# Integer addition in the conversion of 64-bit weights: DeltaNet and SwiGLU on one NeuronCore

## The chip, the cores and the metric

The kernel runs on one core of one Trainium2 chip. The metric is the device time of one launch in microseconds. A core has five engines with queues of their own: TensorE (PE in the profile; its weight loads are PEld), VectorE (DVE), ScalarE (ACT), GpSimd (POOL) and SyncE (SP), which only issues DMAs here.

## The reference

```python
def _attn_ref(q, k, v, beta):                  # q, k, v: (4, 8, 768, 48), beta: (4, 8, 768)
    k_n = k / (np.linalg.norm(k, axis=-1, keepdims=True) + 1e-06)
    state = np.zeros((B, H, D, D))
    for t in range(S):
        y[:, :, t] = np.einsum('bhd,bhde->bhe', q[:, :, t], state)
        v_old = np.einsum('bhde,bhd->bhe', state, kt)
        state = state + bt * np.einsum('bhd,bhe->bhde', kt, vt - v_old)

def _moe_ref(x, w_gate, w_val, w_out, rms_g):  # x: (3072, 384), d_ff = 1536
    rms = np.sqrt(np.mean(x * x, axis=-1, keepdims=True) + 1e-06)
    xn = x / rms * rms_g
    g = xn @ w_gate
    return (g / (1 + np.exp(-g)) * (xn @ w_val)) @ w_out
```

The output of the attention, with the heads of a token put side by side, is `x`. The three weight matrices arrive as 64-bit floats and are used as 32-bit ones, so the kernel has to convert 18 tiles of 768 numbers in each of 128 partitions. q, k, v and beta are 32-bit.

## The kernel before

**Chunks.** The sequence is cut into 12 chunks of 64 steps (`C = 64`), with all 32 heads and both halves of the batch in one chunk. The recurrence within a chunk becomes the inverse of a triangular matrix, built from products of keys. Per chunk, `norms`, `prep`, `qpart` and `recur` do this:

- `norms`: squares (ScalarE), sums (L557, VectorE), a root by power on POOL (L560), the reciprocal (VectorE). L629 scales the keys, on VectorE in chunk 0 and on POOL behind it.
- `prep`: transposes of the keys, their products (L538), a copy to DRAM (`dkk`) and a reload as `at`, in which each partition holds one block of a triangle. `scale` (L654) multiplies it by beta; 15 steps of a product and a sum (L701, L707) invert it. The result goes to DRAM (`dx`, from the buffer `wsum` in the first two chunks) and returns as `mt` and `x2bd`. Matmuls at L759, L783 and L807 merge the halves of the inverse, with copies such as L772 to `m1bd` between them.
- `recur`: products with the state (L849), the new values (L895), the output (L909), the state's update (L946), the root mean square of the output (L977, L983, and on POOL L995 and L996), its scaling (L1011), the transposes to `xf` or `xp1` (L1017) and their copies (L1021).

The first ffn matmul of chunk 0 is at L1084. For chunks 0 and 1 `ffn_plain` multiplies by the weights (L1084 up, L1066 down). For the other ten chunks the up product goes through fewer products of combined factors (L1177, with the combinations in `extra` and `w_in`), and L1234 does the down product. L1334 issues fillers: matmuls without a result, which the planner puts into TensorE's idle time before the time `until`.

**The weights.** `weights` puts 18 tiles into the plan, in order n = 0 to 17: gate and val tiles of `w_in` and tiles of `wo_sb`. A DMA on SP loads tile n into one of three buffers (`raw[n % 3]`), which lie in the large tile `more`. Even n are converted through parts of `xf` and `tmp`, odd n through parts of `more`. With `low` and `high` the two 32-bit halves of a 64-bit float:

- L465, ScalarE: `high` is read as a 32-bit float, scaled and put through Prelu into `top`.
- L453, VectorE: the bits of `top` are shifted left by three.
- L456, VectorE: sign and exponent of that are cut out into `cc`.
- L461, VectorE: `low` (an integer) times 2^-52 times `cc`, which is what the lower half adds.
- the sum of `top` and `cc`. For n below `NPE = 3` TensorE adds the two by matmuls with the identity (L478, L479) and ScalarE copies the result out of PSUM (L483). For the others VectorE adds them (L486).

**The order of the work.** Nothing above is issued in the order of the code. `Plan.add` notes each step with its engine, an assumed duration, a priority, and the keys that it reads and writes. `Plan.run` then simulates all queues 60 times (`forward`), takes new priorities from a pass from the end (`backward`) plus a little noise, keeps the best order, and issues the steps in it. Banks of PSUM and the fillers are assigned in that order too. The weight DMAs have due times of their own (`after`, in L444). DMAs of chunk 0's `prep` are spread over ScalarE's and SP's queues (L645, L649, and `turns` at L730); those of chunk 1 go to SP alone. An engine's queue runs in the planned order and waits at every step for what it needs. So whatever changes a step's engine or assumed duration can move any other step.

## Time and profile before

| what | value |
|---|---|
| timed runs | 711.06, 712.31, 715.30 us (median 712.31) |
| profiled execution, span from first to last instruction | 711.6 us |
| mean granted TensorE clock of the profiled execution | 0.995 |
| busy: TensorE, VectorE, ScalarE, POOL | 98%, 77%, 45%, 19% |
| first ffn matmul, L1084 | 74.01 us |
| conversion of weights, first Prelu to last sum | 13.0 to about 143.9 us |
| L453, L456, L461, L486 on VectorE, each of 128x768 | 0.55, 0.56, 0.96, 0.955 us |
| L465 on ScalarE | 0.93 us |

The page lists no time of the profiled execution other than its span; the shortest timed run is 0.5 us shorter than it and the median 0.7 us longer. Busy shares are of the whole span. The stages differ: up to 74 us only the inversions, the first products and the fillers run, and from there to the end matmuls of the ffn and of later chunks follow one another. Times are from the start of the span.

### The profile page before, as it was taken

Reading aid. Unit: us, or ns where it says so; the run is one execution under the profiler, and the core shown is the slowest. Engines: PE = TensorE matmul, PEld = TensorE weight load, DVE = VectorE, ACT = ScalarE, POOL = GpSimd, SP = SyncE. Lnnn points to the kernel's source line nnn. Section 1 sums busy time; section 2 is a strip of 40 time slices with the busy share of each in tenths; the row PEclk is TensorE's granted clock in tenths of the full one; section 3 lists DMA queues with packets and bytes.
Section 4 is the critical chain, followed back from the end, with each engine's and each line's share of the span. In section 5 each row is a group of like instructions: output and inputs, shape, how many; then the busy total and the mean of one; then the engine's idle time right before and its main releaser. Section 6 shows DMA issues by size and latency. Waiting matters only on the chain.

```text
span 711.6 us, 23292 instructions
## 1 busy us (share of the span) xinstructions
PE 698.8 (98%) x10036; PEld 634.8 (89%) x10036; DVE 545.9 (77%) x1139; ACT 317.7 (45%) x755; POOL 135.4 (19%) x140
## 2 busy tenths in 40 slices
PE   8998998999999999999999999999999999999997
PEld 5656777777799999999999999999999998999997
DVE  4899998999648959938959948946969847976473
ACT  5435553334244445546435355345355355234441
POOL 4201203102021232223130405005040304000000
PEclk9999998999999999999999999999999999999999
DMA  7777895431351261271161262154161161040000
GB/s 138 214 156 179 221 247 137 59 62 35 51 103 25 47 111 34 55 125 34 30 114 25 46 120 51 26 99 85 17 113 17 37 99 33 13 65 2 23 1 23
DMA packets 210071, 54.67 MB, mean 77 GB/s; under 512 B 199216, under 2 KB 202288, under 8 KB 209968
## 3 DMA queue, kind: packets, MB, share of 16 engines
q1 hardware_dynamic: 205120, 52.26, 36.8%
q10 hardware_dynamic: 4848, 0.92, 0.8%
q8 instruction: 79, 1.29, 0.7%
q14 instruction: 24, 0.20, 0.1%
HBM read 40.83 MB, written 12.32 MB: 75 GB/s over the span
## 4 chain that ended last, share of the span: by engine, by line
PE 89%; DVE 6%; DMA 2%; POOL 1%; ACT 1%; issue 1%; POOLq 0%; ACTq 0%; DVEq 0%
PE bank L1177 38%; PE bank L1234 20%; PE bank L1084 9%; PE bank L1066 4%; PE bank L849 3%; PE bank L538 3%; PE bank L515 3%; PE bank L909 2%; DVE acc L707 2%; PE bank L895 2%; PE bank L1334 1%; PE bank L1017 1%; DVE acc L701 1%; PE bank L946 1%; PE bank L783 1%; PE bank L807 1%
## 5 line engine op out<-in xcount | busy, mean ns | idle before, releaser
L1187 DVE TENSOR_TENSOR tmp<-tmp,bank 128x512 f32<-128x512 f32 x180 | 122.2, 685 | 88.6 <-PE bank L1177 63.0
L1177 PE MATMUL bank<-xf,w_in 128*128 128x128 f32 x1440 | 182.0, 277 | 0.0
L1177 PEld LDWEIGHTS bank<-xf,w_in 128*128 128x128 f32 x1440 | 170.1, 192 | 2.6 <-issue 1.2
L1177 PE MATMUL bank<-xf,more 128*128 128x128 f32 x960 | 123.9, 277 | 0.0
L1177 PEld LDWEIGHTS bank<-xf,more 128*128 128x128 f32 x960 | 115.1, 192 | 1.5 <-issue 0.4
L1189 ACT COPY tmp<-bank 128x512 f32<-128x512 f32 x120 | 68.7, 584 | 65.4 <-PE bank L1177 57.2
L707 DVE TENSOR_REDUCE acc<-acc 128x30 f32<-128x90 f32 (+4 forms) x180 | 85.0, 472 | 6.2
L1193 ACT ACTIVATE tmp<-tmp 128x256 f32<-128x256 f32 x120 | 49.5, 417 | 74.5 <-DVE tmp L1187 74.0
L701 DVE TENSOR_TENSOR acc<-acc,at 128x60 f32<-128x60 f32 (+4 forms) x180 | 63.1, 351 | 2.6
L1234 PE MATMUL bank<-wo_sb,hf 128*128 128x192 f32 x360 | 63.9, 328 | 0.0
L1194 DVE TENSOR_TENSOR hf<-tmp 128x256 f32<-128x256 f32 x120 | 53.9, 463 | 12.6 <-ACT tmp L1193 11.4
L560 POOL TENSOR_TENSOR knrm<-ksum,half 128x16 f32<-128x16 f32 x12 | 36.5, 3043 | 121.3 <-DVE ksum L559 121.3
L1234 PEld LDWEIGHTS bank<-wo_sb,hf 128*128 128x128 f32 x360 | 58.1, 190 | 0.5 <-DVE hf L1194 0.2
L1334 PE MATMUL bank<-ident 128*128 128x128 f32 (+2 forms) x156 | 45.2, 437 | 1.4 <-POOL ident masks.py:199 1.4
L1334 PEld LDWEIGHTS bank<-ident 128*128 128x128 f32 x156 | 26.3, 197 | 18.9 <-issue 16.4
L654 POOL TENSOR_TENSOR at<-at,beta_b 128x1024 f32<-128x1024 f32 x8 | 18.9, 2364 | 117.0 <-DMA at<-dkk 94.7
L728 POOL COPY acc<-acc 128x128 f32<-128x128 f32 x40 | 16.5, 445 | 129.2 <-DVE acc L707 128.5
L1084 PE MATMUL bank<-xf,w_in 128*128 128x256 f32 x144 | 33.6, 384 | 0.5 <-ACT xf L1021 0.5
L1084 PE MATMUL bank<-xp,w_in 128*128 128x256 f32 x144 | 34.0, 394 | 0.0
L1066 PE MATMUL bank<-wo_sb,hf 128*128 128x384 f32 x96 | 33.6, 490 | 0.0
L1084 PEld LDWEIGHTS bank<-xp,w_in 128*128 128x128 f32 x144 | 28.1, 198 | 4.4
L1084 PEld LDWEIGHTS bank<-xf,w_in 128*128 128x128 f32 x144 | 26.7, 190 | 5.1 <-ACT xf L1021 0.7
(166 smaller groups left out, 1018.8 us busy)
## 6 DMA issues: line engine op xcount, KB each, us to landing
at<-dkk SPq DMA_DIRECT2D x23, 256.0 KB, 4.2
q<-in_q_dram SPq DMA_DIRECT2D x24, 192.0 KB, 3.8
more<-in_moe_w_val_dram SPq DMA_DIRECT2D x6, 768.0 KB, 6.1
more<-in_moe_w_gate_dram SPq DMA_DIRECT2D x6, 768.0 KB, 6.6
more<-in_moe_w_out_dram SPq DMA_DIRECT2D x6, 768.0 KB, 7.3
vt<-in_v_dram SPq DMA_DIRECT2D x24, 192.0 KB, 4.5
out_dram<-tmp SPq DMA_DIRECT2D x48, 96.0 KB, 2.2
k<-in_k_dram SPq DMA_DIRECT2D x23, 192.0 KB, 4.2
```

The source lines that it names most:

```text
L560: P.add("POOL", 2.95, lambda: nc.gpsimd.tensor_tensor(out=knrm[i2], in0=ksum[i2], in1=half, op=ALU.pow), pn, r=[("ksum", i2), "half"], w=[ ...
L701: nc.vector.tensor_tensor(out=acc[:, 1:3, 0:n, j + 2 : W].rearrange("p a i t -> p i a t"), in0=acc[:, old, 0:n, j : j + 2, None].to_broadc ...
L707: nc.vector.tensor_reduce(out=acc[:, new, 0:n, j + 2 : W], in_=acc[:, lo : lo + 3, 0:n, j + 2 : W].rearrange("p a i t -> p i t a"), axis=A ...
L1066: nc.tensor.matmul(po[p].t[:, 0:DM], hf[:, spot(f), 128 * p : 128 * p + 128], wo_sb[:, spot(f)], start=(f == f0), stop=(f == f1 - 1), skip ...
L1084: nc.tensor.matmul(ps.t[:, TOK * side : TOK * side + TOK], w_in[:, side, h_, 3 * t + i_, n : n + 128], x_[:, 2 * t : 2 * t + 2].rearrange( ...
L1177: nc.tensor.matmul(g.t[:, 128 * z : 128 * z + 128], fac[:, side, 128 * f : 128 * f + 128], xf[:, xs], start=(begin and z == 0), stop=False ...
L1187: P.add("DVE", V(512), lambda t=t, g=g: nc.vector.tensor_tensor(out=t, in0=t, in1=g.t, op=ALU.add), -1, r=[g], w=[tk], last=g)
L1189: P.add("ACT", A(512), lambda t=t, g=g: nc.scalar.copy(t, g.t), -1, r=[g], w=[tk], last=g)
L1193: P.add("ACT", A(256), lambda t=t: nc.scalar.activation(out=t[:, 0:256], in_=t[:, 0:256], func=ACTF.Silu), -1, w=[tk])
L1194: P.add("DVE", V(256), lambda t=t, f0=f0, p=p: nc.vector.tensor_tensor(out=hf[:, spot(f0) : spot(f0) + 2, 128 * p : 128 * p + 128], in0=t[ ...
L1234: nc.tensor.matmul(g.t[:, 0:192], a_[:, f], b_[:, f], start=(begin and f == 0), stop=(f == 5), skip_group_check=True)
L1334: nc.tensor.matmul(warm[:, 0 : 128 * w_].rearrange("p (w n) -> p w n", n=128), ident, ident[:, None, :].to_broadcast([128, w_, 128]))
```

## The change

For every tile the lower word is no longer multiplied by the cut-out exponent on VectorE. ScalarE scales it by 2^-29 and writes it as a 32-bit integer (`rest`, in place of `cc`). VectorE shifts the upper word as before and adds the two as integers, straight into the weights. The path through TensorE for the first three tiles, the mask and the product are gone, and with them the wait of the first down product (`down`, L1096) for the identity matmuls. Everything is planned anew from the new durations, so the order of all queues changes; the due times of the weight DMAs stay.

```diff
-    NPE, NRAW, NCV = 3, 3, 2
+    NRAW, NCV = 3, 2
...
-            top, cc = cva[a], cvb[a]
-            u = top.bitcast(U32)
+            top, rest = cva[a].bitcast(U32), cvb[a].bitcast(U32)
...
-            def s4(u=u, cc=cc):
-                nc.vector.tensor_scalar(
-                    out=cc.bitcast(U32), in0=u, scalar1=0xFF800000, scalar2=None, op0=ALU.bitwise_and
-                )
-            def s5(low=low, cc=cc, by=2.0**-52):
-                nc.vector.scalar_tensor_tensor(out=cc, in0=low, scalar=by, in1=cc, op0=ALU.mult, op1=ALU.mult)
...
+            def shifted(top=top):
+                nc.vector.tensor_scalar(out=top, in0=top, scalar1=3, scalar2=None, op0=ALU.logical_shift_left)
+            def added(dst=dst.bitcast(U32), top=tiled(top), rest=tiled(rest)):
+                nc.vector.tensor_tensor(out=dst, in0=top, in1=rest, op=ALU.add)
...
-            P.add("DVE", 0.57, s2, pr, w=cak)
-            P.add("DVE", 0.57, s4, pr, r=cak, w=cvk)
-            P.add("DVE", 0.96, s5, pr, r=[("raw", i)], w=cvk)
-            if n < NPE:
...
-                    P.add("PE", 0.0035 * m, s6, pr, r=cvk + cak + ["ident"], w=[("cvp", n, x_)], ps=ps, size=8)
...
+            P.add("ACT", 0.84, lambda low=low, rest=rest: nc.scalar.activation(out=rest, in_=low, func=ACTF.Copy, scale=2.0**-29), pr, r=[("raw", i)], w=cvk)
+            P.add("DVE", 0.57, shifted, pr, w=cak)
+            P.add("DVE", 0.97, added, pr, r=cvk + cak, w=done)
...
-                P.add("PE", 0.0, lambda: None, start, r=xk + [("cvp", n, x_) for n in range(NPE) for x_ in range(2)], w=["po"], ps=po[1])
+                P.add("PE", 0.0, lambda: None, start, r=xk, w=["po"], ps=po[1])
```

In the changed kernel the lines behind these are 25 lower: L1084 is L1059 there, L1017 is L992, L654 is L629.

More of the change, by code (lines that the diff above doesn't have):

```diff
@@ L446, in weights @@
             low, high = (raw[i].bitcast(U32)[:, w_ : w_ + 2 * WCOL - 1 : 2] for w_ in range(2))
-            top, cc = cva[a], cvb[a]
-            u = top.bitcast(U32)
+            top, rest = cva[a].bitcast(U32), cvb[a].bitcast(U32)
             tiled = lambda t: t.rearrange("p (a n) -> p a n", a=parts)
             cak, cvk = [("cva", a)], [("o", 1)] if a else [("tmp", 1), ("tmp", 2)]
-            def s2(u=u):
-                nc.vector.tensor_scalar(out=u, in0=u, scalar1=3, scalar2=None, op0=ALU.logical_shift_left)
@@ L455, in s4 @@
-            def s4(u=u, cc=cc):
-                nc.vector.tensor_scalar(
-                    out=cc.bitcast(U32), in0=u, scalar1=0xFF800000, scalar2=None, op0=ALU.bitwise_and
-                )
-            def s5(low=low, cc=cc, by=2.0**-52):
-                nc.vector.scalar_tensor_tensor(out=cc, in0=low, scalar=by, in1=cc, op0=ALU.mult, op1=ALU.mult)
-            P.add("ACT", 0.84, lambda high=high, top=top: nc.scalar.activation(out=top, in_=high.bitcast(FP32), func=ACTF.Prelu, scale=2.0**-112, alpha=2.0**32), pr, r=[("raw", i)], w=cak)
@@ L466, in weights @@
-            P.add("DVE", 0.57, s2, pr, w=cak)
-            P.add("DVE", 0.57, s4, pr, r=cak, w=cvk)
-            P.add("DVE", 0.96, s5, pr, r=[("raw", i)], w=cvk)
-            done = []
-            if n < NPE:
-                for x_ in range(2):
-                    ps = Group()
-                    cut = slice(2 * x_, 2 + x_)
-                    flat = slice(512 * x_, 512 + 256 * x_)
-                    m = 512 - 256 * x_
-                    def s6(ps=ps, top=top[:, flat], cc=cc[:, flat], m=m):
-                        nc.tensor.matmul(ps.t[:, 0:m], ident, top, start=True, stop=False)
-                        nc.tensor.matmul(ps.t[:, 0:m], ident, cc, start=False, stop=True)
-                    P.add("PE", 0.0035 * m, s6, pr, r=cvk + cak + ["ident"], w=[("cvp", n, x_)], ps=ps, size=8)
-                    done.append(("cv", n, x_))
-                    P.add("ACT", A(m), lambda dst=dst[:, cut], ps=ps, m=m: nc.scalar.copy(dst, ps.t[:, 0:m].rearrange("p (a n) -> p a n", n=256)), pr, r=[("cvp", n, x_)], w=[done[-1]], last=ps)
-            else:
-                done.append(("cv", n))
-                P.add("DVE", 0.97, lambda dst=dst, top=tiled(top), cc=tiled(cc): nc.vector.tensor_tensor(out=dst, in0=top, in1=cc, op=ALU.add), pr, r=cvk + cak, w=[done[-1]])
@@ new lines, in shifted @@
+            def shifted(top=top):
+                nc.vector.tensor_scalar(out=top, in0=top, scalar1=3, scalar2=None, op0=ALU.logical_shift_left)
+            def added(dst=dst.bitcast(U32), top=tiled(top), rest=tiled(rest)):
+                nc.vector.tensor_tensor(out=dst, in0=top, in1=rest, op=ALU.add)
+            P.add("ACT", 0.84, lambda high=high, top=cva[a]: nc.scalar.activation(out=top, in_=high.bitcast(FP32), func=ACTF.Prelu, scale=2.0**-112, alpha=2.0**32), pr, r=[("raw", i)], w=cak)
@@ L487, in weights @@
+            P.add("ACT", 0.84, lambda low=low, rest=rest: nc.scalar.activation(out=rest, in_=low, func=ACTF.Copy, scale=2.0**-29), pr, r=[("raw", i)], w=cvk)
+            P.add("DVE", 0.57, shifted, pr, w=cak)
+            done = [("cv", n)]
+            P.add("DVE", 0.97, added, pr, r=cvk + cak, w=done)
             for key in keys:
```

## The prediction

> **What bounds the kernel now.** I read the page's first two parts, then the chain that ended last, then busy time by stage, then the groups of the conversion lines, and last the timeline of each engine around the places where TensorE stood still.

> ```profile
> PE 698.8 (98%) x10036; PEld 634.8 (89%) x10036; DVE 545.9 (77%) x1139; ACT 317.7 (45%) x755; POOL 135.4 (19%) x140
> PE   8998998999999999999999999999999999999997
> PEclk9999998999999999999999999999999999999999
> ```

> TensorE is busy all the time. Ahead of the first ffn matmul (L1084 at 74.01 us, T0 from here on) a part of that is fillers (L1334), which produce nothing; behind T0 it is real work with few holes: 0.34 (near 109), 1.94 (110.2 to 112.14), 0.37 (115.5) and 1.27 us (595.6). So the end is T0, plus a fixed amount of matmul work, plus holes, plus what a lowered clock costs. VectorE decides T0 and the start of what I call T1, the transposes at 112.14. Busy time by stage (PE, PEld, DVE, ACT, POOL, clock) shows its load:

> ```profile
> 40.00:60.00 20.00, 19.21 (x170) 11.10 (x168) 18.83 (x37) 7.09 (x15) 0.00 (x0) 1.00 0.77 183
> 100.00:120.00 20.00, 17.93 (x359) 13.72 (x356) 18.37 (x37) 9.28 (x22) 6.97 (x4) 0.83 0.87 195
> 200.00:300.00 100.00, 99.97 (x1708) 96.67 (x1708) 78.86 (x173) 48.56 (x117) 24.02 (x22) 1.00 0.33 63
> ```

> The chain (start, duration, what) shows which conversions lie on the path: one ahead of chunk 1's inversion (46.06 to 49.73), and one ahead of the norms that lead to T1:

> ```profile
> 46.06 0.70 ACT xf L465
> 46.79 0.57 DVE xf L453
> ...
> 48.05 0.97 DVE tmp L461
> 49.02 0.02 issue
> 49.04 0.69 DVE wo_sb L486
> 49.73 0.19 issue
> 49.92 1.23 DVE at L654
> ...
> 101.58 0.48 DVE more L453
> ...
> 105.78 3.15 POOL knrm L560
> ...
> 109.86 1.59 POOL rs L996
> ```

> The wait at T1 is the one place where the clock falls. PE's windows (length, busy, clock in the fourth column):

> ```profile
> 108.00:110.00 2.00, 1.86 (x128) 1.00 0.73 136
> 110.00:112.00 2.00, 0.21 (x14) 0.98 1.06 243
> 112.00:114.00 2.00, 1.86 (x22) 0.50 1.05 415
> ```

> It stays at 0.5 from 111.93 to 118.76, so 6.83 us do the work of 3.4: that hole costs 1.94 + 3.4 us. The holes of 0.95 (57.13), 1.08 (65.94) and 1.27 us did not lower it.

> **The change, part by part.**

> *Engine time.* Prices are medians from the groups of the conversion lines: Prelu L465 0.93, shift L453 0.55, mask L456 0.56, product L461 0.96, sum L486 0.955 us. VectorE loses mask and product and keeps the shift; for tiles 3 to 17 that is 15 x 1.51 = 22.7 us. Tiles 0 to 2 had no sum on VectorE and get one, so 3 x (1.51 - 0.955) = 1.7: together 24.4 us less. ScalarE gets 18 new passes; no row has this operation, the nearest is L465 over the same 128x768 words: 18 x 0.93 = 16.7, less the six copies L483 (3 x (0.58 + 0.37) = 2.9), so +13.9. TensorE loses 12 identity matmuls, all ahead of T0 where fillers stand in.

> *The new sum* is an integer sum, and no row shows one. The nearest below is L486 (same bytes, 0.955 us). The built instruction works on 16-bit halves, 1,536 elements a partition; at the pace of L654 (1,024 elements, 1.22 us) that is about 1.75 us. I take 0.955 for equal bytes, and keep 1.75 for the range. [...]

> *Less work is not less time by itself.* 13 of the 18 conversions end after 50 us, beside TensorE's queue. Between 120 and 200 TensorE was 100% busy in every window, so what VectorE saves there is worth nothing. A gain can only arise ahead of T0 and in the hole of T1.

> *Chunk 0's inversion.* In the order that the planner now writes, ScalarE does its new pass for tile 1 ahead of its two dkk DMA issues (13.96 us before). The value tile's load, and the reload at (landed 24.46 and 24.69), stand behind those. Everything of chunk 0 moves by one pass, less ScalarE's slack: +0.75. The conversion that also ended there (24.74) gets shorter, but the DMA ended within 0.05 us of it, so nothing comes off.

> *Chunk 1's inversion* (L654 at 49.92) waited for VectorE's conversions of three tiles (8.4 us from 41.5) and for the DMA landing at 49.68, together. The new order puts tiles 2 to 5 there, 4 x 1.51 = 6.0 us. But the new ScalarE pass of tile 5 is queued behind ScalarE's own mt and x2bd issues. Before, those held ScalarE from 46.10 to 49.9 and 52.49 to 53.3; its next instruction sat idle 6.58 us. So the pass ends at 51 to 52, its sum about 1 us later: the inversion starts +1 to +3 later, I take +2.6.

> *What follows in chunk 1.* m1bd's copy (L772) is planned one inversion step earlier (one step near it: 0.42 + 0.58 us). That returns 1.0: the merge L783 (58.19) comes +1.65 (0 to +2). Before the ffn, six transposes now run together and a block of fillers is gone (four fillers' time near 70 us, about 0.95). T0: +1.65 - 0.95 = +0.7 (-0.9 to +1.1).

> *TensorE's cover of that wait.* Before, matmul work and fillers reached up to 0.79 us ahead of L783. Now the identity matmuls are gone (2.6 us a tile), and the filler columns laid out are 3,072 ahead of the merge; at 1.70 ns a column 5.2 us. From about 51 to 52 us they run out 1.6 to 2.8 us before the merge. That is a second hole of the size that lowered the clock at T1 (below, rival B).

> *The k transposes of chunk 2* now stand on TensorE 4.85 us behind T0, in order ahead of the ffn. They need POOL's scaled k (L629), that needs VectorE's norms (L557), which are queued behind the sum of tile 8, which waits for its new ScalarE pass. By the same rows that is ready about 6.5 us behind T0, less what VectorE saves: a stall of 0.3 to 1.7, I take 0.8.

> *T1.* Before, VectorE's conversion (3.07 us) and the norms pow (POOL, 3.15) lay ahead of chunk 1's root L995/L996. Now the roots come ahead of pow. What is left between the last L909 matmul and the transposes is L977 (1.01), L983 (1.13 to 1.22), the root (0.77 + 1.59) and L1011 (0.62): 5.3 us with the hops. The cover that TensorE has in its new order is L946 (0.75) and the scores (1.09): the hole is 5.3 - 1.84 = 3.46 against 1.94, +1.5. The clock then falls as it did, which changes nothing.

> *The loads.* On SP's queue chunk 1's wsum<-dx goes behind three weight loads and is issued near 82.5 instead of 75.62; it lands near 90. In the new order TensorE reaches its reader L759 only near 95, so it costs nothing; where it stood before (86.80) it would cost 3.

> *Row groups.* Behind T0 TensorE has 152 changes of row group instead of 148; each lengthened the record behind it by 0.09 to 0.14 us in the trace, so +0.5.

> Sum: 0.7 + 0.8 + 1.5 + 0.5 = +3.5 us on a span of 711.6, 715.1. The timed median (712.31) is 0.7 above the span, so 715.8.

> **The rivals.** About 0.5% (3.6 us, so 708.7 and 715.9) is what a measurement of this kernel can tell from no change.

> *A, the sum above*: 715.8 (own range 713.5 to 717.2). For: the path after the change is set by DMA landings, ScalarE's queue and POOL, not by VectorE's busy time. Chance 0.38, half of it just under the bound and half over it.

> *B, slower: a second half-clock stretch, ahead of T0.* The price is 6.83 us at half speed; of those 3.4 us about 1.1 fall on fillers, so T0 moves by 2.3 more: 718.1. It decides when the hole ahead of L783 is longer than what the clock tolerates, which the rows put between 1.27 and 1.94 us; my estimate for the hole is 1.6 to 2.8. Against it: L654 may be less late than +2.6, and then the hole closes. [...] Chance 0.24.

> *C, faster: VectorE's relief reaches T1.* The chain names a conversion of 3.07 us ahead of the norms and T1; the new one has 1.51, so that chain shortens by 1.5 and the hole to 0.4, under what lowered the clock: -1.5 - 3.4 = -4.9, with +0.7 at T0 and +0.5 for row groups 708.6; if also the inversion starts on its DMA landing (T0 -0.9), 707.0. Against: with the norms moved, the rest of that chain (5.3 us) doesn't contain VectorE's conversions any more, and TensorE's order has only 1.84 us of cover. Chance 0.22.

> *D, the sum of integers runs at 1.75 us.* Four of them lie ahead of chunk 1's inversion, of which two are not hidden by the waits: +1.6, so 717.4. Chance 0.06.

> *E, nothing moves*: the later inversion is swallowed by the earlier m1bd copy, the k stall is nil and T1's hole is as before: 712 to 713. Chance 0.10.

> **How the numbers follow.** Faster by over 0.5%: C, 0.22. Within: half of A (0.2) and E, 0.30. Slower: B, D and the rest of A, 0.48. The prediction is A's 715.8. For 8 in 10 I keep A, B's middle (to 719.5), E, and of C all down to 707.0.

> **What would show it.** In the changed kernel's profile: the new sum's group (0.955 or 1.75 us); the groups of the new ScalarE pass (0.93); L654's second start on VectorE (51 to 53, not 49.9) with ScalarE's DMA issues ahead of tile 5's pass; TensorE's idle time ahead of chunk 1's merge and the PEclk digits near 55 to 62 us (B); the first ffn matmul near 74.7 (A), near 77 (B) or 73 (C); an idle time named after POOL k some 5 us behind it; the idle time ahead of chunk 1's transposes, near 3.5 (A) or 0.4 (C), and one or no fall of the clock behind it. I am wrong if T0 is earlier than 73, if T1's hole closes, or if the time behind T1 differs from before by more than the row-group term.

## The result and the profile after

The changed kernel took 719.21 us (median of 7 runs, 715.7 to 722.11), the kernel before 713.85 (median of 7, 711.06 to 715.3). The ratio is 1.0083, with a 95% interval of 1.0057 to 1.0109: slower by 0.8%, or 5 to 6 us (the medians are 5.4 apart). The profiled execution has a span of 717.5 us (before 711.6), a mean clock of 0.990 (0.995) and a time of 719.21, 1.7 above its span.

First the page's parts 1 and 2, then the new sum's group.

```profile
PE 700.4 (98%) x10020; PEld 632.9 (88%) x10020; DVE 520.8 (73%) x1106; ACT 328.5 (46%) x767; POOL 139.9 (19%) x140
...
PE   8996997999999999999999999999999999999997
...
PEclk9998998999999999999999999999999999999999
```

```profile
L455 DVE CUSTOM_DVE_ANT_0 w_in<-more x6: 951/958/959, 15.4 to 113.5; 128x1536 uint16<-128x1536 uint16 x6
```

VectorE lost 25.1 us of work (545.9 to 520.8), as planned, and the new sum costs 0.957 us, where 0.955 was taken for it. TensorE, which sets the time, is idle for more of the slices from 54 to 72 us and from 108 to 126 us (each slice is 17.9 us long). The clock falls in both; before, it fell in the second alone. The chain that ended last (start, duration, what) names the places:

```profile
17.41 7.47 DMA at<-dkk
...
24.90 1.24 DVE at L629
...
50.45 0.91 ACT more L458
...
51.39 0.04 DVE w_in L455
51.43 0.84 issue
52.27 1.23 DVE at L629
...
59.32 0.65 PE bank L758 x32
...
68.44 2.69 issue
71.13 0.80 PE bank L921 x18
...
112.90 5.20 issue
```

L629 is the scaling ahead of an inversion (L654 before), L758 the merge (L783), L921 the state's update (L946). The first inversion starts when it did. The second, chunk 1's, is 2.35 us late, behind ScalarE's new pass and the sum. "issue" says that TensorE stood still for no wait that the profile shows; before, such a stop was there too, in L946, 0.88 us long. TensorE's timeline (start, duration, what, and in brackets the idle time before it and what ended it) has the hole ahead of chunk 1's merge, the stop in the state's update with ten filler records behind it, the late first ffn matmul, and the large stop. That one lies in the middle of one block of matmuls, chunk 2's scores.

```profile
59.32 0.65 PE L758 MATMUL bank<-m1bd,kk 128*32 128x64 f32 x32 [2.94 <-DVE m1bd L747]
...
71.13 0.80 PE L921 MATMUL bank<-u,k 64*48 64x48 f32 x26 [2.69 <-issue]
71.86 3.68 PE L1309 MATMUL bank<-ident 128*128 128x512 f32 x10
...
78.63 1.68 PE L1059 MATMUL bank<-xf,w_in 128*128 128x256 f32 x7
...
112.01 0.89 PE L513 MATMUL bank<-qt,kt 64*64 64x64 f32 x47
118.10 0.71 PE L513 MATMUL bank<-qt,kt 64*64 64x64 f32 x17 [5.20 <-issue]
118.74 1.54 PE L992 MATMUL bank<-ident,yn 128*128 128x128 f32 x6
```

Before, the stop in the state's update and the fillers behind it were these:

```profile
67.02 0.69 PE L946 MATMUL bank<-u,k 64*48 64x48 f32 x42 [0.88 <-issue]
67.64 2.43 PE L1334 MATMUL bank<-ident 128*128 128x512 f32 x10
```

The clock (fourth column of PE's windows: length, busy, clock) follows each hole:

```profile
56.00:58.00 2.00, 0.38 (x4) 1.00 1.03 412
58.00:60.00 2.00, 0.68 (x33) 1.00 1.18 293
60.00:62.00 2.00, 2.00 (x21) 0.69 0.61 87
62.00:64.00 2.00, 2.00 (x4) 0.50 0.94 173
...
114.00:116.00 2.00, 0.00 (x0) 0.84 1.07 288
116.00:118.00 2.00, 0.00 (x0) 0.50 1.01 162
```

It was at 0.5 from 60.76 for 3.41 us, from 71.00 for 3.41, and from 115.38 for 6.83; before, once in the work, from 111.93 for 6.83.

What is TensorE waiting for? Part 3 of the page lists an instruction queue of 78 packets and 1.28 MB, so 16 KB each:

```profile
q8 instruction: 78, 1.28, 0.8%
```

The trace has 20,040 records of TensorE (10,020 matmuls and as many weight loads), 257 for every packet. The DMA view of two windows, first 110.7 to 115.6, then 115.6 to 117 (packets, MB, share of 16 engines):

```profile
q1 hardware_dynamic: 467, 1.11, 101.2%
```

```profile
q1 hardware_dynamic: 1158, 0.30, 118.6%
q8 instruction: 1, 0.02, 5.2%
```

In the first 2.7 us of the stop, from 112.90 on, the queue of data has 101.2% of the DMA engines' time, and no instruction packet is served. One comes at 115.64 and takes 1.18 us, and 1.3 us behind its end TensorE goes on. The stop in the state's update ends in the same way: a packet at 68.52 takes 1.15 us, and 1.5 us behind its end TensorE goes on. Between the two stops lie 1,526 of TensorE's records, and the second packet is the sixth behind the first, so 254 records for each. If the packets are spaced like that throughout (an estimate, by a count over the trace's records), none is served earlier than some 295 records before TensorE would run dry; at the rate of L884, L921 and L513 (351 records from 110.32 to 112.68, 149 a microsecond) these last 2 us. My theory F (fetch) was therefore that the two stops are instruction fetches queued behind data. Theory O (order) was that the loss as a whole comes from the order that was planned anew, and not from the conversion.

### The profile page after: what moved, and what is told of

The parts are those of the page before. It is cut to its first block, busy times and chain, and to the rows that moved or that the text cites. A ratio compares the mean times of both kernels' runs of the same rounds, so it can differ in the third digit from the quotient of the medians.

```text
span 717.5 us, 23183 instructions
## 1 busy us (share of the span) xinstructions
PE 700.4 (98%) x10020; PEld 632.9 (88%) x10020; DVE 520.8 (73%) x1106; ACT 328.5 (46%) x767; POOL 139.9 (19%) x140
## 3 DMA queue, kind: packets, MB, share of 16 engines
q8 instruction: 78, 1.28, 0.8%
## 4 chain that ended last, share of the span: by engine, by line
PE 91%; DVE 4%; DMA 2%; issue 2%; ACT 1%; POOL 0%; ACTq 0%; POOLq 0%
PE bank L1152 39%; PE bank L1209 19%; PE bank L1059 9%; PE bank L1041 5%; PE bank L824 3%; PE bank L513 3%; PE bank L490 3%; PE bank L1309 2%; PE bank L884 2%; PE bank L870 2%; DVE acc L682 1%; PE bank L921 1%; PE bank L992 1%; DMA at<-dkk 1%; PE bank L782 1%
## 5 line engine op out<-in xcount | busy, mean ns | idle before, releaser
L1152 PEld LDWEIGHTS bank<-xf,w_in 128*128 128x128 f32 x1440 | 170.0, 192 | 2.8 <-issue 1.2
L1152 PEld LDWEIGHTS bank<-xf,more 128*128 128x128 f32 x960 | 115.4, 192 | 1.8 <-issue 0.2
L1168 ACT ACTIVATE tmp<-tmp 128x256 f32<-128x256 f32 x120 | 49.9, 418 | 81.8 <-DVE tmp L1162 81.5
L1169 DVE TENSOR_TENSOR hf<-tmp 128x256 f32<-128x256 f32 x120 | 50.5, 433 | 9.2 <-ACT tmp L1168 8.5
L1309 PE MATMUL bank<-ident 128*128 128x512 f32 (+2 forms) x164 | 55.5, 490 | 1.4 <-POOL ident masks.py:199 1.4
L1309 PEld LDWEIGHTS bank<-ident 128*128 128x128 f32 x164 | 29.9, 205 | 25.6 <-issue 23.0
L703 POOL COPY acc<-acc 128x128 f32<-128x128 f32 x40 | 22.0, 580 | 103.2 <-DVE acc L682 102.5
L629 POOL TENSOR_TENSOR at<-at,beta_b 128x1024 f32<-128x1024 f32 x8 | 19.2, 2397 | 99.6 <-DMA at<-dkk 99.6
L1041 PE MATMUL bank<-wo_sb,hf 128*128 128x384 f32 x96 | 35.3, 504 | 0.0
L1059 PE MATMUL bank<-xf,w_in 128*128 128x256 f32 x144 | 34.1, 384 | 0.0
L1059 PE MATMUL bank<-xp,w_in 128*128 128x256 f32 x144 | 32.9, 381 | 0.0
L1218 DVE TENSOR_TENSOR tmp<-tmp,bank 128x192 f32<-128x192 f32 x30 | 10.5, 350 | 30.0 <-PE bank L1209 28.9
L1059 PEld LDWEIGHTS bank<-xp,w_in 128*128 128x128 f32 x144 | 27.0, 190 | 4.5
```

The lines of the kernel that those rows point to most:

```text
L1041: nc.tensor.matmul(po[p].t[:, 0:DM], hf[:, spot(f), 128 * p : 128 * p + 128], wo_sb[:, spot(f)], start=(f == f0), stop=(f == f1 - 1), skip ...
L1059: nc.tensor.matmul(ps.t[:, TOK * side : TOK * side + TOK], w_in[:, side, h_, 3 * t + i_, n : n + 128], x_[:, 2 * t : 2 * t + 2].rearrange( ...
L1152: nc.tensor.matmul(g.t[:, 128 * z : 128 * z + 128], fac[:, side, 128 * f : 128 * f + 128], xf[:, xs], start=(begin and z == 0), stop=False ...
L1168: P.add("ACT", A(256), lambda t=t: nc.scalar.activation(out=t[:, 0:256], in_=t[:, 0:256], func=ACTF.Silu), -1, w=[tk])
L1169: P.add("DVE", V(256), lambda t=t, f0=f0, p=p: nc.vector.tensor_tensor(out=hf[:, spot(f0) : spot(f0) + 2, 128 * p : 128 * p + 128], in0=t[ ...
L1309: nc.tensor.matmul(warm[:, 0 : 128 * w_].rearrange("p (w n) -> p w n", n=128), ident, ident[:, None, :].to_broadcast([128, w_, 128]))
```

## The experiments

Except for old_order, before_warm and light_loads, each takes the changed kernel's planned order and moves the steps named, after the planner is done; hole_filled moves none and adds fillers. MOVES names the step that is moved, by its number in the plan, and the step that it goes before or after. The edit that does this is the same in all:

```diff
-        for op, s in best[1]:
+        line = list(best[1])
+        for a, where, b in MOVES:
+            x = next(o for o in line if o[0].n == a)
+            line.remove(x)
+            y = next(k for k, o in enumerate(line) if o[0].n == b)
+            line.insert(y + (where == "after"), (x[0], line[y][1]))
+        for op, s in line:
```

**old_order.** The plan is made with the old steps and the bodies are exchanged.

```diff
+            def both(high=high, top=top, low=low, rest=cc.bitcast(U32)):
+                nc.scalar.activation(out=top, in_=high.bitcast(FP32), func=ACTF.Prelu, scale=2.0**-112, alpha=2.0**32)
+                nc.scalar.activation(out=rest, in_=low, func=ACTF.Copy, scale=2.0**-29)
...
+            P.add("ACT", 0.84, both, pr, r=[("raw", i)], w=cak)
...
-            P.add("DVE", 0.96, s5, pr, r=[("raw", i)], w=cvk)
+            P.add("DVE", 0.96, added if n < NPE else s5, pr, r=[("raw", i)], w=cvk)   # the bodies of s4 and s5 are empty
```

> The new conversion (ScalarE's second pass, one shift and one integer sum on VectorE, for all 18 tiles) put into the order of the kernel before: the plan is made with the old steps, and their bodies are exchanged, so every other step stays where it was. The 12 identity matmuls stay as fillers of the same size. Theory O (the loss is in the order that was planned anew): chunk 1's inversion starts near 49.9 us, chunk 1's merge is not late by more than about 0.9, one fall of the clock at most, and the time is 711 to 714, a ratio to the kernel before of 0.995 to 1.002. Theory C (the conversion itself costs it, by ScalarE's longer queue): 717 or more, ratio over 1.005, with steps late behind ScalarE's passes.

Measured: 711.9, ratio 0.9989 (0.9965 to 1.0013). The same conversion in the old order costs nothing that can be told, so the loss of 0.8% is the order's. What it brings is visible too: in VectorE's timeline chunk 1's inversion starts at 48.87 and waits only for its DMA.

```profile
48.87 1.23 DVE L659 TENSOR_TENSOR at<-at,beta_b 128x1024 f32<-128x1024 f32 x1 [2.27 <-DMA at<-dkk]
```

What takes it back stands in the chain and in TensorE's timeline. ScalarE's first mt transfer, issued at 45.51, takes 6.92 us to land, and SP issues the next one only then. TensorE's first merge step waits 1.24 us for that. The clock is at half from 55.95 for 3.41 us, so the eight filler records take 3.96 us, where they took 2.43 before, and the merge came at 59.12 instead of 58.19.

```profile
45.51 6.92 DMA mt<-dx
...
52.45 1.70 DMA mt<-dx
```

```profile
54.20 1.10 PE L764 MATMUL bank<-ident,mt 32*32 32x32 f32 x62 [1.24 <-DMA mt<-dx]
```

**act_first.** One step moved in ScalarE's queue.

```diff
+MOVES = [(56, "before", 174)]     # 56: pass L458 of tile 5; 174: ScalarE's first mt<-dx
```

> The changed kernel with one step moved: ScalarE's new pass of tile 5 goes ahead of ScalarE's mt and x2bd DMA issues. Theory O: the inversion (L629) starts on its DMA landing, 50 to 50.5 instead of 52.27; the hole ahead of the merge L758 shrinks from 2.94 to about 1, the first fall of the clock (60.76) goes, the first ffn matmul comes 3 to 4 us earlier, and the time falls by 2 to 4 us against the changed kernel. Rival (the inversion waits for the landing of at and not for the sum): L629 stays at 52, no gain, and 0.9 us of loss because the DMA issues are late.

Measured: 713.01, ratio 0.9977 (0.9956 to 0.9999), so 1.1% less than the changed kernel's ratio, or 6 to 8 us, where I had expected 2 to 4. The inversion starts at 47.98, 4.3 us earlier than in the changed kernel and 1.9 earlier than before; my 50 was too late, because the reload had landed sooner than I thought. All engines:

```profile
46.07 0.94 ACT L468 ACTIVATE more<-more 128x768 uint32<-128x768 uint32 x1
...
47.05 0.96 DVE L465 CUSTOM_DVE_ANT_0 w_in<-more 128x1536 uint16<-128x1536 uint16 x1 [0.22 <-ACT more L468]
...
47.98 1.23 DVE L639 TENSOR_TENSOR at<-at,beta_b 128x1024 f32<-128x1024 f32 x1
```

The first ffn matmul comes at 70.38 (78.63 in the changed kernel, 74.01 before) without a fall of the clock ahead of it; the stop in the state's update is 0.15 us there (2.69 in the changed kernel), so the gain isn't the inversion's alone. The 3.6 us gained by then on the kernel before are lost again in the scores: the stop there is now 6.50 us, and the clock is at half for 10.24, so the profiled spans are 711.5 and 711.6.

**hole_filled.**

```diff
+EXTRA = {191: [4, 4, 4, 2]}       # 191: merge L758; four fillers ahead of it
...
+            if filler and op.n in EXTRA:
+                filler(EXTRA[op.n])
```

> The changed kernel with four more fillers (1,792 columns, 3.05 us) ahead of chunk 1's merge L758, in the hole of 2.94 us. Nothing else moves. If that hole lowers the clock at 60.76 us, the fall goes, what follows the merge takes 1.7 us less, and the time falls by 1 to 2 us. If the clock falls for another reason, it stays and the time is the same or 0.3 us longer.

Measured: 717.94, ratio 1.0058 (1.0037 to 1.0079), some 2 us less than the changed kernel, though the intervals overlap. In the profile the falls at 60.76 and at 71.0 are both gone, and the first ffn matmul is at 75.5. The stops are the better finding. TensorE's timeline:

```profile
67.02 0.53 PE L931 MATMUL bank<-u,k 64*48 64x48 f32 x30
69.45 0.60 PE L931 MATMUL bank<-u,k 64*48 64x48 f32 x34 [1.90 <-issue]
...
108.88 0.77 PE L523 MATMUL bank<-qt,kt 64*64 64x64 f32 x39
115.97 0.92 PE L523 MATMUL bank<-qt,kt 64*64 64x64 f32 x25 [6.31 <-issue]
```

They came behind 38 and 47 records of their blocks; they now come behind 30 and 39. Four fillers are eight matmul records. Counted from the start over matmuls and weight loads, the stops stand behind record 1,461 and 2,987 in the changed kernel and here, and in light_loads and spread_right as well. So in these four profiles the stops are tied to a number of TensorE's records and not to a step of the program, as F has it and a wait for a step would not.

**light_loads.** The rest of the weights of tiles 7 to 17 is left out.

```diff
+            if n >= 7:
+                c8 = src.shape[2] // 8
+                rdst, src = rdst[:, :, 0:c8], src[:, :, 0:c8]
```

> The changed kernel, but the weight loads of tiles 7 to 17 move an eighth of their bytes (the rest of those tiles keeps old data, so that part of the weights is left out). Order and instruction counts stay. Theory F (TensorE stands still inside L921 at 68.4 and inside L513 at 112.9 because its next 256 instructions are fetched by a DMA that queues behind the data): both stalls, 2.69 and 5.20 us, fall under 1 us, the clock's falls at 71.0 and 115.4 become shorter or go, and the time falls by 4 to 9 us. Rival (these stops come from something that TensorE waits for, a bank or a semaphore that the profile doesn't name): they stay at 2 us or more, and the time falls by no more than what earlier landings give, 0 to 2 us.

Measured: 711.41, ratio 0.9964 (0.995 to 0.9978), 1.2% under the changed kernel's. The stops stay at the same instructions, but are 0.52 and 1.41 us, the second longer than the 1 us that I gave it.

```profile
69.10 0.52 PE L924 MATMUL bank<-u,k 64*48 64x48 f32 x26 [0.52 <-issue]
...
110.74 0.47 PE L516 MATMUL bank<-qt,kt 64*64 64x64 f32 x17 [1.41 <-issue]
```

The fall of the clock at 60.6 remained (its hole has another cause), that at 71 went, that behind the scores was 3.41 instead of 6.83. F holds: less data, shorter stops, same place (where the expectation has 256 instructions, the runs have 257 records of TensorE for a packet over the whole span, and 254 between the stops). Here conversions could also start earlier; spread_right, below, moves all the bytes.

**spread_loads, first_spread, first_both.** Four weight loads moved in SP's queue.

```diff
+MOVES = [(99, "before", 285), (104, "before", 359), (109, "before", 420), (114, "after", 697)]   # tiles 14 to 17
```

> The changed kernel, whole, with four weight loads moved in SP's queue and nothing else: tile 14 ahead of the second four wsum<-dx, tile 15 ahead of dkk<-kk, tile 16 ahead of vt, tile 17 behind the k loads. The same bytes move, but fewer of them between 104 and 116 us. Theory F (the stop of 5.20 us inside L513 is an instruction fetch behind data): that stop shrinks to under 2.5 us, chunk 1's transposes come 2 us earlier than 118.8, and the time falls by 2 to 4 us against the changed kernel; the stop inside L921 at 68.4 us, where the loads are as before, stays over 1.5 us. Rival (it waits for something else, or the light loads helped by earlier conversions only): the stop stays near 5 and the time within 1 us of the changed kernel.

> act_first (ScalarE's pass of tile 5 ahead of its DMA issues) with the four loads moved as in spread_loads. Theory O with F: the first ffn matmul stays near 70.4, the stop of 6.50 us inside the scores shrinks to under 3, the clock's fall there (10.24 us) becomes 6.83 or 3.41, and the time is 3 to 6 us under the kernel before. If the loads don't matter: as act_first, about 1.6 under it.

> act_first with the moved loads and the moved scores. Where both repairs act on the same wait, it is no better than the better one of them by more than 1 us: 4 to 7 us under the kernel before.

Measured: ratios 1.0104 (1.0086 to 1.0122), 1.0069 (1.0051 to 1.0087) and 1.0072 (1.0054 to 1.0091): all slower, against my numbers. The stop in the scores did shrink to 1.27 us in the first of them. But I had put tile 15's load one step too early, ahead of ScalarE's second pass of tile 12, which reads the buffer that it fills. In these three, tile 12 gets the low words of tile 15, and ScalarE waits for that load:

```profile
98.15 0.89 ACT L468 ACTIVATE tmp<-more 128x768 uint32<-128x768 uint32 x1 [8.45 <-DMA more<-in_moe_w_val_dram]
```

Chunk 1's merge waits for what is queued behind it, 3.4 us, and the clock falls there. By their times they tell nothing on whether the move pays.

**spread_right**, the same with that load behind the pass.

```diff
+MOVES = [(99, "before", 285), (104, "after", 362), (109, "before", 420), (114, "after", 697)]
```

> spread_loads mended: tile 14's load ahead of the second four wsum<-dx, tile 15's and 16's right behind dkk<-kk, behind every pass that reads the buffers they fill, tile 17's behind the k loads. All bytes move, in an order without the wait of 8.45 us. Theory F: with one load early and one late, fewer bytes are under way when the fetch is asked for (near 110 us), the stop of 5.20 us inside the scores shrinks to 1 to 3.5, the transposes come 1.5 to 3 us earlier than 118.7, and the time falls by 1 to 4 us against the changed kernel. Rival: the stop stays near 5 us.

Measured: 717.03, ratio 1.004 (1.0012 to 1.0068), about 0.4% or 2 to 3 us under the changed kernel, though the intervals overlap. With all its bytes moved, the instruction packet is served 3 us earlier (112.56, 115.64 in the changed kernel) and the stop is 1.83 us, as F has it. The stop in the state's update, near which no load was moved, stays at 2.35. The clock still falls three times, for 10.24 us behind the scores, and the profiled span is 718.0:

```profile
115.44 0.46 PE L523 MATMUL bank<-qt,kt 64*64 64x64 f32 x17 [1.83 <-issue]
```

**first_later.** act_first, and in TensorE's queue the down product ahead of the scores, and these behind the transposes.

```diff
+MOVES = [(56, "before", 174), (461, "before", 426), (426, "after", 340)]   # 426: scores; 340: transposes
```

> act_first with two steps moved on TensorE instead: the down product behind the transposes goes ahead of chunk 2's scores, and these go behind chunk 1's transposes. The fetch then arrives while TensorE waits for the transposes' input anyway: they come at about 108.4 instead of 111.8, and the time is 3 to 5 us under the kernel before. If the stop is tied to the scores themselves it moves with them, the transposes are early all the same, and the gain is 0 to 2 us against act_first.

Measured: 711.62, ratio 0.9965 (0.9949 to 0.9982). The transposes came at 109.03 (expected 108.4), the stop in the scores fell to 0.65, but the 2.36 us in which TensorE waits for the transposes' input lowered the clock for 10.24 us: 2.5 under the kernel before, not 3 to 5.

**first_warm, first_warm17, first_all.** Fillers in that hole, written to the bank that the transposes use next; then tile 17's load behind the k loads; then all four loads as in spread_right.

```diff
                 def xtr(p=p, psx=psx):
+                    if c == 1 and not warmed:
+                        warmed.append(p)
+                        for w_ in [4, 4, 2]:
+                            nc.tensor.matmul(psx.t[:, 0 : 128 * w_].rearrange("p (w n) -> p w n", n=128), ident, ident[:, None, :].to_broadcast([128, w_, 128]))
```

> first_later with three fillers (1,280 columns, 2.18 us) in the hole of 2.36 us ahead of chunk 1's transposes; they write to the bank that the transposes are about to use. Theory H (what the hole costs is mostly the clock's fall behind it: 10.24 us at half speed, 5.1 us): the fall goes, and the time is 4 to 5 us under first_later, 6 to 8 under the kernel before (ratio 0.989 to 0.992). Rival (the stop of 0.65 us inside the scores, or the fetch, lowers it as well): a fall of 3.41 us or more stays and the gain is under 3 us.

> first_warm with the load of tile 17 moved behind the k loads in SP's queue, so that 768 KB less are under way between 102.6 and 108 us. Theory F: the fetch asked for at 103.7 lands one to two us earlier and the stop of 0.65 us inside the scores goes; at most 1 us less than first_warm. If something waits for tile 17 (converted near 118 us), up to 2 us more.

> first_warm (tile 5's pass first, the scores behind the transposes, fillers in the hole) with these four loads moved. As first_warm17 if only tile 17's load mattered (ratio 0.995); 1 to 2 us better if the early load of tile 14 helps the fetch too; worse by 1 us or more if it delays chunk 1's wsum<-dx.

Measured: 712.52, ratio 0.9978 (0.9957 to 0.9999); 709.12, 0.9948 (0.9918 to 0.9978); 708.59, 0.9935 (0.9909 to 0.996). The fillers alone brought nothing: a stop of 1.46 us in the scores and a fall of 6.83 us took their place. With tile 17's load out of the way too, the scores run through and the clock stays up in the profile. In first_all:

```profile
109.04 1.05 PE L1010 MATMUL bank<-ident,yn 128*128 128x128 f32 x6 [0.21 <-ACT yn L998]
110.02 1.16 PE L523 MATMUL bank<-qt,kt 64*64 64x64 f32 x64
```

first_all is the best version that I ran, 0.65% under the kernel before; whether tile 14's early load helps beyond tile 17's late one is not settled (the intervals overlap).

**before_warm.** Two fillers in the same place of the kernel before ([4, 4] in the edit above).

> The kernel before with two fillers (1,024 columns, 1.74 us) in its own hole of 1.94 us ahead of chunk 1's transposes, for a fair comparison. Theory H: the one fall of the clock (6.83 us) goes and the time falls by 3 to 3.5 us, ratio near 0.995. Then first_warm is ahead of it by what the conversion brings in the mended order, 3 to 4 us. If the fillers run into something that TensorE needs, no gain.

Measured: 712.83, ratio 0.9998 (0.9969 to 1.0028), no gain. The clock did not fall in the profile, but a stop of 1.53 us stood in the scores, and with the fillers behind it the transposes were 1.8 us later than before (113.94).

## Why the prediction was wrong

719.2 lies within 707.0 to 719.5, but the 715.8 rested on case A and lay, by the prediction's own bound of 715.9, just inside what can't be told from no change; the result is clear of that. The profiled span grew by 5.9 us, not 3.5. Another 1.5 us of the miss is the base: the sum stood on a median of 712.31 for the kernel before, and the seven runs above give 713.85.

The step that failed is T0, put at +0.7 us; it came out at +4.62. The prediction gave the hole ahead of chunk 1's merge no price in the clock, and had no term for the stop in the state's update. By stage: up to T0 +4.62 (forecast +0.7), from T0 to T1 +1.98 (forecast +2.3), behind T1 -0.70 (forecast +0.5). The second agrees by luck, as the items on it show.

- *The conversion's prices*: right. Sum 0.957, new pass 0.90 to 0.92 us (0.93 taken). Rival D is out. The 0.955 was an estimate from equal bytes, and it holds here: 1,536 16-bit elements took 0.957 us, 768 32-bit ones in L486 0.955.
- *Chunk 0's inversion*, +0.75: wrong, 24.90 against 24.94. ScalarE's extra pass did not hold up its dkk issues: they start at 13.98, before at 13.96, while the pass runs.
- *Chunk 1's inversion*, +2.6: right, +2.35, and for the reason given; act_first took it away by that one step.
- *The merge*, +1.65: +1.13, so the direction was right and the size a third less.
- *The hole ahead of it*: 2.94, my estimate 1.6 to 2.8. Here the choice failed: I saw that this was over the 1.94 us which had lowered the clock, and still gave that outcome (rival B) 0.24 and the forecast to A. The clock fell, though for 3.41 us and not 6.83; hole_filled, which fills the hole, has no fall there. The bounds that the choice went by, 1.27 and 1.94 us, don't hold either: in old_order 1.24 us of waiting were enough. The three falls of the changed kernel's profile start at 60.76, 71.00 and 115.38, which is 3 and 13 times 3.41 us apart, and in the 3.41 us ahead of each TensorE was idle for 2.0 to 2.6.
- *T0*, +0.7: wrong, +4.62 (78.63), and the step that decides. Of it 1.13 is the merge. The stop in L921 adds 1.8 (2.69 us against 0.88 before). The two falls of the clock add some 3.3 by my estimate from the rows between: 3.41 us of nearly full work at half speed each, so the eight filler records behind the merge take 3.36 us (2.00 before) and the ten behind the stop 3.68 (2.43). What goes the other way, fewer fillers and shorter waits, is the rest, about -1.6. The fetch of instructions was in none of my terms or rivals, though 0.88 us of "issue" inside L946 stood in the chain of before.
- *The k transposes*, 0.8: wrong, there was no stall.
- *T1's hole*, 3.46 for POOL's chain: TensorE stood 5.20 us inside the scores, longer than the chain, whose result was ready near 116.5; the transposes came at 118.74. Without the stop the scores would have ended near 113.6, and the hole to 116.5 would have been 2.9 us (an estimate), so the chain's price was near. The cause was wrong: the scores were taken for cover, and they were what stood still. That the stage came near its +2.3 is luck: the stall of the k transposes did not come, and the stop did.
- *Row groups and the rest behind T1*, +0.5: -0.7. It hardly moved, but "the clock falls as it did, which changes nothing" was not why. The fall is 6.83 us long as before, but 3.4 of these had passed when the transposes started (0.2 before), most of them in the stop. So some 1.6 us less is lost behind T1 (an estimate), and what the row groups cost can't be told.
- *C*, faster: it did not come in the planned order, but its idea was half right. In an order without the late pass the inversion starts 1.9 us earlier than before (act_first), and the first ffn matmul comes 3.6 earlier, where C had 0.9.

Over all runs, most of the loss goes with a lower clock. Span times mean clock (what the span would be if the clock's loss were all on the path) has a median of 709.7 in 86 runs of the kernel before and of 710.5 in 7 of the changed one; the median span is 712.3 and 717.5. By this measure 0.8 of the 5.2 us lie outside the clock. It gives the clock too much, as it also counts the half-clock time in which TensorE stood still (2.7 us of the last fall). In the two profiles TensorE's idle time grew by 4.3 us (12.8 to 17.1), and its busy time, longer at a lower clock, by 1.6.

What stays open: how much of the gain of act_first or first_all over the kernel before is VectorE's and how much the order's; no run gave the old conversion an order without holes and stops.

## What to carry to other kernels

A replanned order can cost more than the operation that is changed saves (719.21 us here, and 711.9 with the same conversion in the old order): freeze the order, exchange the bodies, and you see which of the two it was. On a queue that issues DMAs as well, look first at a compute step planned behind them when a step with less work comes later: tile 5's pass, put ahead of ScalarE's mt transfers in act_first, brought chunk 1's inversion forward by 4.3 us. And price a hole on TensorE by the clock behind it, not only by its length (1.94 us of waiting and 6.83 us at half speed in the kernel before), and ask of a block of small matmuls beside large loads whether its instructions arrive in time (a stop of 5.20 us in the changed kernel, 1.41 in light_loads).
